# One product for the scores of both batch rows of a tile, and a re-searched issue order

## The chip, the cores and the metric

The kernel runs on one core of a Trainium2 chip. The metric is the time of one launch on the device in microseconds (us). A core has a matrix engine (PE in the profile, with its weight loads listed as PEld), a vector engine (DVE), a scalar engine (ACT), GpSimd (POOL) and a queue engine that issues transfers (SP). Each engine executes its own list of instructions in order, and semaphores hold an instruction back until what it needs is there.

## The reference

Two blocks follow each other. The first is a recurrence over 768 steps, for 4 batches and 8 heads, with a state of 40 x 40:

```python
y[:, :, t] = np.einsum('bhd,bhde->bhe', rt, state)
Sa = np.einsum('bhde,bhe->bhd', state, at)
state_decay = state * wt[:, :, None, :] - np.einsum('bhd,bhe->bhde', Sa, bt)
state = state_decay + np.einsum('bhd,bhe->bhde', vt, kt)
```

Its output, laid out as 3072 tokens of 320 channels, goes through a gated feed-forward block with 1536 inner channels:

```python
xn = x / np.sqrt(np.mean(x * x, axis=-1, keepdims=True) + 1e-06) * rms_g
out = silu(xn @ w_gate) * (xn @ w_val) @ w_out
```

The inputs of the recurrence are float32; everything on the chip is computed in float32.

## The kernel before

**Chunks.** The sequence is cut into 24 chunks of C = 32 steps. For a chunk, `front(c)` loads the inputs, turns them and builds the decayed keys of five levels (blocks of 1, 2, 4, 8 and 16 steps); `inverse(c)` solves a triangular system on DVE; `main(c)` applies the solution, updates the state, forms the chunk's outputs `y` and normalises them. Chunks are collected into 13 groups (one, then eleven times two, then one), and `feed(g)` sends a group's tokens (128 or 256 columns) through the feed-forward weights. `narrow` converts these weights from 64-bit words once, near the start.

**The scores.** A tile of 128 partitions holds two halves. In the turned operands `vut` and `rE` the partition half `o` (partitions 0 to 39 and 64 to 103) and the slot `n` (eight of them) together tell which of 16 sequences of a pair of batches it is, and `i` tells which pair. The two `i` sit side by side along the free dimension, as the two batch rows of a tile, with 64 columns of `vut` for each. The step that the change touches, `pe("score", ...)` in `main`, multiplies for each of the 8 x 2 x 2 combinations of `n`, `i`, `o` a stationary block of `vut` of 40 x 64 by a moving block of `rE` of 40 x 32 (32 time steps), and writes 64 partitions by 32 columns. After it, the levels' masked copies `As` are made from these scores: for each of the five levels, DVE (`tt`) or ACT (`scale`) multiplies the score columns of that level by the mask `msi`. `msi` is indexed by the partition half and by `i`, and is zero where the two don't belong together. The `level` products that follow, 16 for each level, multiply `As` by the keys and give the chunk's own part of `y`.

**Products and records.** A float32 product appears in the profile as two PE records with a weight load each, and a transpose (`flip`) as one with one load. So the 32 products of a chunk's scores are 64 records, 1536 in all. Products whose operands lie on different partition halves, or whose outputs do, work on different tiles of the matrix engine.

**The order.** Nothing is issued where it is written. Each call records a step (`plan.add`) with what it needs, 5999 steps in all, of which 1093 are groups of PE products. At the end `plan.issue(ORDER, PAIRS)` issues all steps in the order of a written list, `ORDER`, each word counting from the first step that is not yet issued. `PAIRS` says which of three pairs of PSUM banks (`ps0` to `ps2`) each use of PSUM gets; a fourth pair, `po`, gathers the feed-forward outputs. On each engine, and on each transfer queue (SP's, POOL's), the list is therefore the order of execution. The list was found by a search outside the kernel.

**Lines in the profile.** Steps are issued through helpers, so the profile's lines are theirs: L531 is every product (`mm`), L534 every transpose (`flip`), L485 the DVE operations, L508, L512 and L515 ACT's, L528 the transfers. The tiles tell steps apart: `ps<-rE,vut` is the scores, `ps<-As,KN` and `ps<-As,kbn` the levels, `ps<-rE,Sd` and `ps<-r,Sd` the state's part of `y`, `ps<-A,K` and `ps<-Ab,K` the products of keys, `ps<-VU,KN` the update of the state, `ps<-xg,wf` and `po<-wf,hT` the feed-forward block, `ps<-ident,...` the transposes.

Of the kernel before, what the change touches and what calls it, by code (L numbers as in the profile page):

```python
# [16 lines left out]
P = 128  # L17
C = 32
# [15 lines left out]
72 66 3 68 69 2 4 200 693 192 46 36 5 6 25 0 0 57 58 195 40 0 53 55 336 51 52 40 63 0 41 69 68 58 359 186 78 79 195  # L34
189 196 46 358 184 379 0 41 0 0 4 45 17 14 16 15 77 367 375 0 0 0 17 18 55 65 47 173 0 18 13 382 360 23 172 56 381
361 675 85 0 351 352 61 353 64 185 173 63 73 76 89 0 76 357 99 4 0 1 21 25 85 70 95 109 97 22 369 370 352 2 86 4 353
0 0 10 362 363 656 165 657 49 3 52 51 80 340 82 357 341 373 58 62 374 346 347 358 67 92 91 359 348 103 366 367 66
360 70 69 63 15 41 40 42 368 349 64 78 77 65 74 94 79 89 88 75 93 85 86 350 59 90 96 97 105 101 76 106 100 108 107
110 167 87 99 649 369 111 351 109 174 175 176 9 156 113 115 114 20 361 352 370 181 375 102 98 22 371 112 385 178 179
182 188 376 377 372 393 192 187 189 193 191 177 204 183 184 378 116 383 403 402 50 289 194 382 117 190 200 384 118  # L40
119 205 120 203 121 163 198 122 123 185 124 199 125 288 126 202 186 127 379 195 211 128 209 129 210 130 380 131 201
215 132 24 405 404 0 169 158 390 210 129 377 420 421 209 130 192 202 204 218 131 203 213 132 391 392 393 133 214 224
134 135 136 223 225 156 222 382 137 138 286 640 212 644 168 139 140 141 142 144 651 394 402 215 383 384 395 385 396
143 227 386 216 397 387 228 226 441 229 403 388 404 405 642 422 423 406 176 424 407 217 289 408 145 440 232 233 425
271 287 641 430 193 643 649 14 659 288 234 235 426 236 429 431 442 272 237 238 239 427 443 149 444 240 219 241 100
242 428 243 221 148 146 664 665 147 273 244 432 433 274 275 434 435 245 445 246 247 446 248 276 277 447 450 451 449
249 452 453 454 250 448 251 436 252 437 253 254 471 472 455 438 255 456 492 281 278 280 491 256 439 482 257 457 258
481 473 279 230 231 290 282 291 650 658 648 646 259 480 474 475 458 260 208 220 261 483 459 283 262 264 265 493 476
494 294 263 302 301 311 299 303 312 295 296 495 763 666 300 298 297 500 501 503 502 477 484 496 304 307 266 0 307
496 673 304 484 269 308 646 485 14 835 819 0 231 46 2 1 0 195 18 22 196 23 186 24 25 469 470 472 368 197 26 187 251  # L50
540 207 371 370 212 198 231 369 381 473 383 375 385 388 376 474 526 525 213 214 27 28 399 386 215 475 476 430 230
398 29 387 410 216 384 217 397 30 396 477 479 481 478 31 480 395 406 530 533 538 539 536 537 250 241 232 218 377 392
378 233 393 394 234 379 484 32 485 252 235 242 240 239 380 389 391 529 527 409 405 408 390 400 407 253 254 364 543 0
0 370 371 203 210 204 368 378 222 384 379 387 389 390 388 393 391 394 392 385 211 205 229 381 212 223 382 380 369
213 455 459 458 383 228 214 224 466 469 516 457 456 215 465 460 462 463 461 468 216 470 225 249 471 464 467 472 398
399 400 401 402 476 403 517 474 0 2 385 403 404 472 476 405 406 407 477 408 409 0 0 395 327 328 396 329 330 331 332
311 312 418 164 428 431 430 429 435 333 334 391 143 142 436 335 336 337 338 339 340 341 545 544 365 415 248 342 343
345 346 344 347 348 349 442 417 446 437 366 397 546 549 548 547 441 529 443 166 167 448 447 438 445 444 439 452 440
456 458 350 351 454 453 457 455 530 449 465 451 414 459 468 464 463 450 146 460 461 469 471 472 482 480 462 467 532
533 434 147 148 470 466 483 481 486 487 168 663 473 149 674 150 151 425 478 534 476 169 152 485 477 484 474 490 424  # L60
535 536 537 170 171 538 539 479 172 173 540 531 475 541 491 492 493 494 495 496 497 498 499 500 369 370 542 676 664
675 681 662 670 665 667 677 671 673 666 543 550 678 551 501 502 503 504 505 506 507 508 509 672 398 399 400 510 680
401 686 511 512 513 687 402 554 555 556 783 185 174 176 514 515 516 517 518 519 520 175 558 177 178 557 523 522 521
524 562 560 563 179 180 564 559 561 181 182 566 565 568 183 184 573 569 567 570 571 525 528 403 527 575 572 574 576
784 577 578 786 186 187 188 579 842 843 841 526 854 580 488 489 682 840 685 844 683 785 189 744 787 788 789 669 697
684 851 839 790 404 581 702 405 407 696 406 190 191 688 192 689 690 847 582 695 700 712 710 713 698 699 724 733 701
791 795 709 711 793 792 583 794 691 798 584 585 721 692 707 693 708 552 694 703 720 732 799 706 719 717 195 194 193
196 197 718 722 723 553 704 714 715 725 729 726 731 705 730 727 716 802 807 728 804 803 736 806 810 813 815 816 805
811 809 198 199 200 0 0 4 6 806 810 815 816 812 584 817 732 733 735 738 820 818 821 5 739 737 736 743 744 745 746
747 1 0 0 737 738 745 746 4 0 0 701 702 773 703 704 628 799 801 797 798 806 617 705 706 774 707 708 770 775 709 776  # L70
777 808 810 952 802 953 811 807 710 814 1078 1075 1082 1073 809 823 1083 711 1085 1072 1074 828 0 0 1087 5 813 0 3 5
0 0 811 4 707 708 822 709 807 808 46 47 48 53 821 816 710 817 819 711 830 52 54 49 712 820 713 0 829 840 0 781 783
782 664 5 665 0 665 790 761 666 762 776 667 670 669 778 777 763 764 773 792 791 789 787 46 0 47 42 43 770 769 44 49
788 783 48 50 45 89 797 663 666 779 781 794 90 780 684 790 791 799 800 798 0 0 0 642 652 710 594 701 384 386 387 1
576 0 10 17 6 785 0 1 650 0 380 700 8 10 573 697 927 638 922 9 2 4 712 11 5 0 698 571 12 14 779 780 782 15 591 592
796 0 792 794 702 700 703 701 568 778 0 0 0 767 768 781 365 769 770 772 773 771 367 366 695 696 697 698 699 700 701
702 703 704 706 705 708 709 710 711 712 713 714 715 716 717 718 719 720 721 722 723 724 725 726 727 728 729 730 0 1
773 782 706 730 602 603 604 605 894 783 370 731 732 733 734 735 736 367 606 372 371 368 373 797 800 799 737 738 739
786 792 740 741 787 788 918 919 905 742 743 744 904 2 789 791 745 369 374 790 793 796 746 798 794 805 795 806 801
912 747 802 748 895 803 804 807 808 809 810 1109 811 914 812 749 1098 1097 0 1102 913 747 748 912 1093 1104 926 931  # L80
749 751 750 752 0 542 546 547 570 558 0 5 0 5 314 550 551 553 554 315 9 0 565 5 6 0 0 552 543 544 561 545 576 558
559 562 564 546 376 378 377 555 557 560 575 574 556 569 570 572 227 573 571 13 595 582 7 12 9 8 10 14 15 566 567 577
578 579 730 568 394 580 585 0 0 0 212 214 213 1 215 379 649 388 389 417 572 570 571 574 575 573 576 418 419 420 524
567 565 421 2 4 580 581 363 585 582 583 587 584 589 586 3 647 648 8 5 591 588 590 593 594 712 505 703 650 592 595
596 597 598 599 600 601 602 364 651 655 653 708 707 704 718 654 7 0 0 0 0 641 647 1 566 592 593 594 595 596 597 598
599 600 601 648 651 657 567 602 656 603 604 605 652 658 606 662 664 665 607 2 7 8 653 4 654 608 655 661 699 504 659
609 660 610 666 611 667 612 9 10 663 668 669 671 670 613 672 614 673 674 615 675 616 676 3 5 617 618 0 671 682 962
487 702 704 6 706 8 613 614 842 0 7 400 698 702 711 610 611 612 613 614 704 615 616 700 617 619 712 705 706 710 715
725 716 618 620 714 959 713 960 958 969 727 723 717 726 707 728 724 9 721 736 708 967 970 838 492 722 709 718 738
737 720 733 719 732 0 6 0 0 0 4 615 617 616 618 728 628 629 723 724 734 735 745 742 743 744 747 749 729 733 737 748  # L90
540 739 746 725 678 688 689 822 395 396 398 397 0 733 731 828 830 747 682 955 829 394 815 816 818 831 957 954 945 0
# [313 lines left out]
def kernel(  # L405
# [41 lines left out]
    N = 8  # L447
    NI = 2 * N
# [38 lines left out]
    def tt(o, a, b, op, more=0.0):  # L487
        dve(0.065, nc.vector.tensor_tensor, o, a, b, op, more=more)
# [359 lines left out]
    def main(c):  # L848
# [61 lines left out]
        for j, l in reversed(list(enumerate(LEVELS))):  # L910
            G = C // (2 * l)
            if G == 1:
                for i in range(2):
                    scale(As[:, j, :, i], sc.rearrange("p o n t -> p (o n) t")[:, :, 16:C], msi[:, j, i, 0:1])
# [183 lines left out]
```

## Time and profile before

| What | Value |
|---|---|
| median of three runs | 1036.21 us (1034.24 to 1039.02) |
| the profiled execution's own time | 1031.24 us |
| its span, first to last instruction | 1029.5 us |
| PE busy | 945.0 us (92%), 24592 products, 24592 weight loads |
| DVE busy | 788.9 us (77%), 2745 instructions |
| ACT busy | 497.8 us (48%), 1113 instructions |
| POOL busy | 301.1 us (29%), 528 instructions |
| mean granted PE clock | 0.952 |
| instruction transfers | 193 packets with 3.16 MB on one queue, 47 with 0.39 MB on another |

A busy PE need not be at its peak: the profile models the end of a product, and a record's length (some 200 ns for a small product) contains time in which the next ones already run. What a group of products costs is therefore read from the start of its first record to the start of the next group's first one.

### The profile page before, as it was taken

The numbers are of one execution on the slowest core, as the hardware profiler recorded it, in microseconds if no ns is written. First come the engines' busy times: TensorE is split into PE (matmuls) and PEld (weight loads), VectorE is DVE, ScalarE is ACT, GpSimd is POOL, SyncE is SP. The second block draws the span as 40 slices with busy tenths as digits, with TensorE's granted clock in tenths as the row PEclk, the third lists the DMA queues.
The fourth block names the chain that finished last, engine by engine and source line by source line (L and its number), as shares of the span: only waits on it lengthen the run. The fifth ranks groups of instructions, "written<-read, shape, count | busy, mean of one in ns | idle before, by whom it ended". The sixth has DMA issues, their size and how long they took to land.

```text
span 1029.5 us, 55521 instructions
## 1 busy us (share of the span) xinstructions
PE 945.0 (92%) x24592; PEld 770.9 (75%) x24592; DVE 788.9 (77%) x2745; ACT 497.8 (48%) x1113; POOL 301.1 (29%) x528
## 2 busy tenths in 40 slices
PE   3557878999999999999999899999999999999998
PEld 2446767877777778777877777777787787787777
DVE  8999977966869778878878678688698788777531
ACT  5676456554463454464454534634534545436131
POOL 9323234211433232333321324123232313400000
PEclk9996555999999999999999999999999999999999
DMA  7664433322242242232331233232322322420100
GB/s 167 152 175 107 109 87 79 61 60 54 47 83 43 49 88 48 55 79 44 67 77 28 60 65 60 55 67 45 78 48 54 78 47 60 75 44 10 42 7 21
DMA packets 147056, 68.89 MB, mean 67 GB/s; under 512 B 121088, under 2 KB 136384, under 8 KB 146816
## 3 DMA queue, kind: packets, MB, share of 16 engines
q1 hardware_dynamic: 128448, 42.37, 18.3%
q0 software_dynamic: 16192, 22.64, 11.5%
q8 instruction: 193, 3.16, 1.3%
q10 hardware_dynamic: 2176, 0.33, 0.2%
q14 instruction: 47, 0.39, 0.1%
HBM read 55.05 MB, written 10.22 MB: 63 GB/s over the span
## 4 chain that ended last, share of the span: by engine, by line
PE 78%; DVE 6%; DMA 6%; issue 5%; SPq 3%; ACT 2%; POOL 0%; DVEq 0%; ACTq 0%; POOLq 0%
PE ps L531 55%; PE po L531 16%; PE ps L534 7%; SPq L528 3%; DMA sB<-LT 1%; DMA M<-sB 1%; DVE Yi L485 1%; DMA LT<-sY 1%; ACT VU L512 1%; DVE wf L485 1%; DVE y L485 1%; DVE tmp L485 1%; DVE LT L485 1%; DMA kbn<-in_b_dram 1%; DMA sY<-Yi 1%
## 5 line engine op out<-in xcount | busy, mean ns | idle before, releaser
L531 PE MATMUL ps<-xg,wf 128*128 128x256 f32 (+3 forms) x1872 | 360.8, 375 | 0.0
L531 PEld LDWEIGHTS ps<-xg,wf 128*128 128x128 f32 (+1 forms) x1872 | 267.7, 190 | 48.7 <-issue 12.5
L531 PE MATMUL po<-wf,hT 128*128 128x320 f32 x576 | 180.8, 448 | 1.5 <-issue 1.3
L531 PEld LDWEIGHTS po<-wf,hT 128*128 128x128 f32 x576 | 103.5, 191 | 38.8 <-issue 4.5
L485 DVE TENSOR_TENSOR hT<-ps,sg 128x256 f32<-128x256 f32 (+1 forms) x156 | 59.9, 399 | 91.0 <-PE ps L531 54.8
L485 DVE TENSOR_TENSOR tmp<-Yi,M 128x24 f32<-128x24 f32 (+21 forms) x512 | 106.9, 209 | 16.8 <-ACT x L508 3.3
L485 DVE TENSOR_TENSOR Yi<-Yi,tmp 128x24 f32<-128x24 f32 (+21 forms) x512 | 106.9, 209 | 10.6
L508 ACT ACTIVATE sg<-ps 128x256 f32<-128x256 f32 (+1 forms) x156 | 54.0, 369 | 110.0 <-PE ps L531 107.0
L528 POOL DMA_DIRECT2D VU<-in_v_dram x92 | 54.1, 590 | 154.0 <-PE ps L531 113.8
L485 DVE TENSOR_TENSOR K<-K,T 128x512 f32<-128x512 f32 (+1 forms) x192 | 92.6, 497 | 4.8 <-PE ps L531 2.7
L531 PE MATMUL ps<-Ab,K 40*60 40x56 f32 (+2 forms) x4608 | 83.3, 232 | 8.6 <-DVE tmp L485 2.4
L531 PEld LDWEIGHTS ps<-Ab,K 40*60 40x60 f32 (+2 forms) x4608 | 76.1, 143 | 17.1 <-issue 8.3
L518 POOL TENSOR_TENSOR ss<-ss,mhalf 128x1 f32<-128x1 f32 x24 | 14.3, 596 | 249.8 <-DVE ss L485 249.7
L512 ACT COPY KN<-ps 128x640 f32<-128x640 f32 x96 | 65.8, 692 | 39.0 <-DVE LT L485 24.7
L528 POOL DMA_DIRECT2D kbn<-in_k_dram x92 | 53.9, 587 | 100.5 <-PE ps L531 99.3
L485 DVE TENSOR_TENSOR As<-ps,msi 128x256 f32<-128x256 f32 (+1 forms) x168 | 70.9, 454 | 15.5 <-PE ps L531 8.7
L528 POOL DMA_DIRECT2D kbn<-in_b_dram x92 | 53.8, 586 | 82.5 <-PE ps L531 80.8
L531 PEld LDWEIGHTS ps<-As,KN 128*40 128x40 f32 x3072 | 67.5, 129 | 12.6 <-issue 4.2
L531 PE MATMUL ps<-As,KN 128*40 128x32 f32 x3072 | 72.7, 208 | 3.5 <-DVE As L485 1.6
L512 ACT COPY K<-K 128x512 f32<-128x512 f32 x96 | 61.0, 635 | 28.6 <-PE ps L531 13.3
L485 DVE SCALAR_TENSOR_TENSOR Yi<-M,Yi 128x31 f32<-128x31 f32 (+6 forms) x228 | 44.4, 243 | 30.8 <-DMA M<-sB 18.5
L528 POOL DMA_DIRECT2D wn<-in_w_dram x92 | 51.8, 564 | 45.3 <-DVE KN L485 45.1
(128 smaller groups left out, 1503.8 us busy)
## 6 DMA issues: line engine op xcount, KB each, us to landing
M<-sB SPq DMA_DIRECT2D x96, 128.0 KB, 3.0
wan<-in_r_dram SPq DMA_DIRECT2D x24, 160.0 KB, 3.7
kbn<-in_k_dram POOLq DMA_DIRECT2D x92, 40.0 KB, 2.4
kbn<-in_b_dram POOLq DMA_DIRECT2D x92, 40.0 KB, 2.8
VU<-in_v_dram POOLq DMA_DIRECT2D x92, 40.0 KB, 3.0
wan<-in_w_dram POOLq DMA_DIRECT2D x46, 80.0 KB, 2.9
wan<-in_a_dram POOLq DMA_DIRECT2D x46, 80.0 KB, 2.8
wn<-in_w_dram POOLq DMA_DIRECT2D x92, 40.0 KB, 2.7
```

What stands on the lines that cost most here:

```text
L485: plan.add("DVE", time + more + each * size(o), 0.087, lambda at: [fn(at(o), *m(at))], [o], aps(*args))
L508: scalar(o, [a], lambda at: nc.scalar.activation(at(o), at(a), f, **kw), aps(acc), 0.1 if f in (AF.Square, AF.Relu) else 0.0)
L512: scalar(o, [a], lambda at: nc.scalar.copy(at(o), at(a)), extra=more)
L518: plan.add("POOL", 0.5, 0.06, lambda at: nc.gpsimd.tensor_tensor(o, a, b, op), [o], [a, b])
L528: plan.add(by, 0.6 if by == "POOL" else 0.45, 0.0, lambda at: queue.dma_start(out=o, in_=i), [o], [i], load=load, since=since)
L531: return o, lhsT, rhs, lambda at: nc.tensor.matmul(at(o), lhsT, rhs, start=start, stop=stop, skip_group_check=True), 4
L534: return o, i, ident, lambda at: nc.tensor.transpose(at(o), i, ident), 2
```

## The change

Two things change, the score products and the written order. The five masked copies read the same number of elements as before, now at the place where the new product puts them.

A score product now takes both batch rows of a slot together: the stationary operand is all 128 columns of `vut` (40 x 128), the moving operand the 2 x 32 steps of both rows (40 x 64), and the output 128 partitions by 64 columns. There are 8 x 2 of them in a chunk in place of 8 x 2 x 2. Half of each output block pairs a partition half with the other row's steps; these cross blocks are finite numbers that nothing needs, and the zeros of `msi` remove them.

```diff
         sc = plan.room().rearrange("p o (n t) -> p o n t", n=N)
-        pe("score", [mm(sc[half(i), o, n, 0:C], vut[part(o), n, half(i)], R["rE"][part(o), n, i, tk])
-                          for n, i, o in each])
+        pe("score", [mm(sc[:, o, n].rearrange("p (i t) -> p i t", i=2), vut[part(o), n], R["rE"][part(o), n, :, tk])
+                     for n in range(N) for o in range(2)])
+        sc = sc.rearrange("p o n (i t) -> p (o n) i t", i=2)
         As = As_.next()
         for j, l in reversed(list(enumerate(LEVELS))):
             G = C // (2 * l)
             if G == 1:
                 for i in range(2):
-                    scale(As[:, j, :, i], sc.rearrange("p o n t -> p (o n) t")[:, :, 16:C], msi[:, j, i, 0:1])
+                    scale(As[:, j, :, i], sc[:, :, i, 16:], msi[:, j, i, 0:1])
             elif l == 1:
-                tt(As[:, j], sc.rearrange("p o n t -> p (o n) t")[:, :, None, 1:C:2].to_broadcast((P, NI, 2, 16)),
+                tt(As[:, j], sc[:, :, :, 1::2],
                    msi[:, j:j + 1].to_broadcast((P, NI, 2, 16)), MUL)
             else:
                 for i in range(2):
                     tt(As[:, j, :, i].rearrange("p n (g l) -> p n g l", g=G),
-                       side(sc.rearrange("p o n t -> p (o n) t")[:, :, 0:C], l, 1),
+                       side(sc[:, :, i], l, 1),
                        msi[:, j:j + 1, i].rearrange("p n (g l) -> p n g l", g=G).to_broadcast((P, NI, G, l)), MUL)
```

The lists `ORDER` and `PAIRS` are replaced as a whole, by the result of a new search; in it the time of an order was a mean over several assumed delays of the blocks in which instructions arrive. The 5999 steps are the same, but for the size of the 24 score steps; only their order and the PSUM pairs differ.

```diff
 ORDER = """
-72 66 3 68 69 2 4 200 693 192 46 36 5 6 25 0 0 57 58 195 40 0 53 55 336 51 52 40 63 0 41 69 68 58 359 186 78 79 195
+71 46 2 4 72 368 200 3 202 0 53 190 54 52 46 4 5 50 6 49 7 78 69 66 76 77 67 0 53 0 38 42 191 194 39 51 55 77 78 357
...
```

## The prediction

> **What bounds the kernel now.** I read the page's busy shares and slices first, then the sums over stretches, PE's waits, and the order of time on PE.
>
> ```profile
> PE 945.0 (92%) x24592; PEld 770.9 (75%) x24592; DVE 788.9 (77%) x2745; ACT 497.8 (48%) x1113; POOL 301.1 (29%) x528
> ...
> PE   3557878999999999999999899999999999999998
> ...
> DVE  8999977966869778878878678688698788777531
> ...
> PEclk9996555999999999999999999999999999999999
> ```
>
> ```profile
> core 0: us, PE busy (x) PEld busy (x) DVE busy (x) ACT busy (x) POOL busy (x), PEclk, DMA share, GB/s
> 0.00:193.00 193.00, 131.12 (x4282) 118.32 (x4282) 168.94 (x507) 113.94 (x227) 76.31 (x145) 0.75 0.52 121
> ...
> 200.00:1000.00 800.00, 781.95 (x19900) 626.31 (x19899) 609.90 (x2196) 374.95 (x859) 219.68 (x375) 1.00 0.27 56
> ```
>
> There are two stages. Up to 193 us DVE is the busiest (168.9 of 193), PE has 61.9 us idle, and its granted clock is mostly half. From 200 to 1000 us PE is busy 782 of 800: work added to PE there moves the end, and at most 18 us of its idle time could take some up. Of these 18 us the waits of a quarter microsecond or more sum to 13.2 for "issue", with nothing in the profile to wait for, and 2.7 for ACT, DVE or DMA. Over the whole span the largest wait is:
>
> ```profile
> PE ps L531 <- issue: 12.9, 19, 1.6
> ```
>
> Last, the order of time on PE at full clock (start, time to the last end, records):
>
> ```profile
> 304.79 0.22 PE L531 MATMUL ps<-rE,Sd 40*40 40x32 f32 x1
> ...
> 305.42 1.11 PE L531 MATMUL ps<-rE,vut 40*64 40x32 f32 x64
> 306.47 4.79 PE L531 MATMUL ps<-xg,wf 64*128 64x256 f32 x24
> ...
> 322.17 1.15 PE L531 MATMUL ps<-A,K 40*64 40x56 f32 x64
> 323.14 1.06 PE L531 MATMUL ps<-Ab,K 40*60 40x56 f32 x64
> ...
> 346.93 1.14 PE L531 MATMUL ps<-rE,vut 40*64 40x32 f32 x64
> 347.89 0.20 PE L531 MATMUL ps<-rE,Sd 40*40 40x32 f32 x1
> ...
> 358.40 0.70 PE L534 MATMUL ps<-ident,K 40*128 40x40 f32 x16
> 359.03 1.13 PE L531 MATMUL ps<-xg,wf 128*128 128x256 f32 x4
> ```
>
> ```profile
> 1003.09 1.16 PE L531 MATMUL ps<-xg,wf 64*128 64x128 f32 x16
> ```
>
> Read from start to next start, 64 records of the scores (40 x 64 stationary, 32 moving columns) take 346.93 to 347.89 = 0.96 us, or 1.05 us at 305.42. The group of y's state part before them has 64 records too, and 32 moving columns, but 40 stationary ones: 304.79 to 305.42 = 0.63 us. The keys' product has 64 stationary and 56 moving columns: 322.17 to 323.14 = 0.97 us. So moving 32 or 56 columns is the same, and 40 or 64 stationary ones is the difference: such groups are bound by loading the stationary operand. The score records start in rounds of four (one for each quarter of the engine) 0.0585 us apart.
>
> **The change part by part.**
>
> 1. The scores' product. A chunk's 64 records become 32, with 128 stationary and 64 moving columns. An output of 128 partitions leaves two tiles (the partition halves), so it is 16 rounds of two in place of 16 rounds of four. The nearest row is the last fence: 64 x 128 stationary, the same two tiles, 128 moving columns; its pairs start 0.112 us apart, and the 16 records hold PE for 1.09 us until the next group's start. Its weight-load records are 0.188 us long against the scores' 0.135, so the load is longer by 0.053, as a round is (0.112 against 0.0585). Sixteen rounds at 0.112 are 1.79 us; with 0.06 for the first I take 1.85. Lower end: transposes of 40 x 128, 16 records in 358.40 to 359.03 = 0.63 us, so 1.26 for 32; but a transpose's load record is 0.138 us, and an ordinary product's isn't. Upper end: the group of 16 twice, 2.18. So +0.86 us a chunk at full clock (from 0.99, the mean of 0.96 to 1.05; +0.27 to +1.19). Twenty of the 24 score groups start after 200 us: +17.2 us (5 to 24).
>
> 2. The first four, at 70, 102, 146 and 176 us, run at half clock, where the group at 146 took 1.87 us; twice +0.86 is 1.7 each, 6.9 in all if nothing covers it, nothing if DVE does. DVE covers most of this stage, so I take +2.
>
> 3. The masked copies. DVE's rows of 256 and 512 elements (416 and 681 ns) and ACT's (471 ns) keep their sizes; only the address changes. Zero, and I see no row that would price a stride. They wait for the scores, 0.9 us longer each; the wait is hidden while PE has other groups to run, as it has after 200 us, and lies on the chain at the first chunks (in 2).
>
> 4. Changes of tile shape. The scores took 0.954 us where the next group has the same tile shape, and 1.044 to 1.066 where it hasn't: 0.1 us a change. Counted in the two written orders, PE goes from 530 changes to 557, since the scores leave the shape of y's products for that of the transposes: +2.7 us.
>
> 5. Blocks of instructions. 193 packets for PE's 49184 records and some 280 others are 256 instructions each, and the "issue" gaps after 200 us fall on every 256th instruction. They come where the 256 before took, by the rows of their groups, under about 3.1 us, and last about what is missing. Summed so, 29 blocks after 200 us lack 18.2 us; the trace shows 18.3 lost at block ends (13.2 of idle, the rest records that start late). In the new order it is 187 blocks, and 30 short ones that lack 20.0 us. I take 0, from -13 (all idle of this kind gone) to +5.
>
> 6. The rest of the order. The steps are the same 5999. Ahead of each score and each group's first feed-forward product stand the same sums of PE work, within 2.6 us, and in the first 200 us of DVE work, within 2 us; nothing is moved by a stage. SP's and POOL's transfers are reshuffled in their queues: POOL waits hundreds of us in all and PE for a transfer hardly at all after 200 us, so that costs nothing unless a load comes late for a turn (9.5 us, once, near 16 us in this trace). Nothing, -6 to +6.
>
> 7. Longer scores give the other engines time: of the 4.8 us (18 less 13.2) in which PE waited for others, I let 4 go.
>
> Sum: 17.2 + 2 + 2.7 + 0 + 0 - 4 = +17.9 us, or 1049 on the profiled execution's own 1031.24. That one is 5 us below the median of the runs, so I add the sum to 1036.21: 1054 us.
>
> **The rivals.**
>
> *The count rules (faster).* If each record cost the same, 32 in place of 64 would halve the group: 0.5 us x 24 = -12, so 1024 us. It decides if the new group takes under 0.96 us. Against it: 0.63 and 0.97 us for equal counts. The Trainium skill states this rule, in "TensorEngine Tiling (Array Packing)", Instruction Overhead: each product carries some 60 cycles, whatever its few moving columns, so a small size should not be split. The trace agrees as to the moving columns (32 or 56: 0.96 and 0.97 us), but not that the records' count alone sets the time. Chance 0.04.
>
> *The load is that of a transpose.* Then +0.27 x 20, with 2.7 for shapes and less for 7: +5, 1041 us. Against it: the load records of 0.188. Chance 0.06.
>
> *The new order wins the time back*, at block ends and at the start: to hide 17 us nearly all of the 18.3 must go. For it: that is what its search averaged over. Against it: 20.0 us by the rows. 1037 us, chance 0.13.
>
> *The clock.* It is granted for good at 193 us. PE is busy 46.5 of 50 us from 150 to 200, so each 10 us that full clock comes earlier there are worth up to 5 us. Granted near 120 us it would give some 30 us, 1024 us (chance 0.06); granted 40 us later, 1074 us (0.05). Longer score groups fill gaps, which may help; no row settles it.
>
> **How the numbers follow.** Forecast 0.66, alone 1044 to 1066 us (items 1 and 5). A change under 0.5% (5 us, about what these runs can tell from none) takes most of the winning order (0.10 of 0.13) and the transposes' load (0.06), less a little: same 0.15. Faster: 0.04 + 0.06 + a tail of 0.01: 0.11. Slower 0.74. The range from 1035 to 1070 leaves out the count, the two clocks and a part of the winning order, 0.18.
>
> **What would show it.** The group `ps<-rE,vut` has 768 records of 40*128 with 64 moving columns, starting in pairs 0.112 us apart and taking 1.8 to 2.0 us to the next group's start; DVE's and ACT's `As` rows are as before; PE's span from 200 us on grows, its share of "issue" waits stays near 13 us. The prediction is wrong if that group takes under 1.3 us, if "issue" waits fall below 5 us, or if the clock is granted far from 193 us.

## The result: 1064 us after 1037, slower by 2.75%, and the profile after

| | before | changed |
|---|---|---|
| median of six runs each, side by side | 1036.97 us (1033.29 to 1039.02) | 1064.43 us (1061.28 to 1071.07) |
| ratio, with its 95% interval | | 1.0275 [1.0239, 1.031] |
| the same, in later runs | 1035.34 us | 1060.87 us, 1.0253 [1.0201, 1.0306] |
| own time and span of the profile read here | 1031.24 and 1029.5 us | 1053.92 and 1052.1 us |

The forecast was 1054 us, +17.9; the medians say +27.5 and +25.5. The first profile of the changed kernel ran at a granted clock of at most 0.949 throughout (span 1069.3 us), so the lines below come from the second, `e0_changed_again`, whose full clock is 1.0. It is the fastest of that kernel's four runs there, by 4.7 us or more, so it holds only part of what the medians show: its span is 22.6 us longer than before's.

From the page of the changed kernel, the busy sums and the 40 slices:

```profile
PE 967.0 (92%) x23824; PEld 792.1 (75%) x23824; DVE 795.1 (76%) x2745; ACT 500.8 (48%) x1113; POOL 303.4 (29%) x528
...
PE   2547888999999999999999999999999999999998
...
DVE  9989998867867867768778688678597687776531
...
PEclk9997665999999999999999999999999999999999
```

PE executes 768 records fewer and is busy 22.0 us longer (967.0 against 945.0), of the 22.6 us by which the span has grown. DVE, ACT and POOL are within 6.2, 3.0 and 2.3 us of before. The sums over stretches (length, then busy time and records of PE, PEld, DVE, ACT, POOL, then granted clock, share of the transfer engines, GB/s):

```profile
0.00:193.00 193.00, 129.28 (x4108) 117.39 (x4110) 172.18 (x496) 112.49 (x222) 76.95 (x143) 0.80 0.50 120
...
200.00:1000.00 800.00, 782.47 (x19048) 629.63 (x19049) 603.85 (x2185) 372.49 (x848) 222.39 (x378) 1.00 0.26 55
1000.00:1053.00 53.00, 48.22 (x598) 39.05 (x596) 12.54 (x36) 12.10 (x35) 0.56 (x1) 1.00 0.07 15
```

From 200 to 1000 us PE was as idle as before: 17.5 us of 800 against 18.1. Longer products did not take up its waits. The largest waits of PE, over the whole span (engine, line, what it waited for: us, times, longest; lines here are one lower than in the kernel before):

```profile
PE ps L533 <- DVE wf L484: 11.6, 1, 11.6
PE ps L530 <- issue: 9.6, 13, 1.7
```

Now the group itself, in the order of time on PE (start, time to the last end, records), and its records by tile (shortest, median, longest in ns), first in the changed kernel:

```profile
308.02 1.98 PE L530 MATMUL ps<-rE,vut 40*128 40x64 f32 x32
309.84 1.08 PE L530 MATMUL ps<-xg,wf 64*128 64x256 f32 x8
```

```profile
L530 PEld LDWEIGHTS ps<-rE,vut x768: 182/188/331, 76.2 to 1014.2; 40*128 40x128 f32 x192
L530 PE MATMUL ps<-rE,vut x768: 258/272/472, 76.2 to 1014.3; 40*128 40x64 f32 x192
```

and the loads in the kernel before:

```profile
L531 PEld LDWEIGHTS ps<-rE,vut x1536: 129/135/228, 70.4 to 990.4; 40*64 40x64 f32 x192
```

Half the records take 1.82 us (308.02 to 309.84), and 1.93 where the next group has another tile shape (390.87 to 392.80), in place of 0.96 to 1.05: the load of 128 columns is 188 ns against 135. The rows of the masked copies (mean ns of one after the bar's busy time) stay where they were, 416, 681 and 471 ns before:

```profile
L484 DVE TENSOR_TENSOR As<-ps,msi 128x256 f32<-128x256 f32 x144 | 55.6, 417 | 31.4 <-ACT As L514 22.8 <-PE ps L530 8.5
...
L484 DVE TENSOR_TENSOR As<-ps,msi 128x512 f32<-128x512 f32 x24 | 16.4, 683 | 2.4 <-PE ps L530 1.8 <-ACT As L514 0.6
...
L514 ACT ACTIVATE As<-ps,msi 128x256 f32<-128x256 f32 x48 | 21.0, 471 | 46.7 <-PE ps L530 33.5 <-DVE As L484 13.2
```

### The profile page after: what moved, and what is told of

Its sections match the earlier page's. It is cut to its first block, busy times and chain, and to the rows that moved or that the text cites. A ratio compares the mean times of both kernels' runs of the same rounds, so it can differ in the third digit from the quotient of the medians.

```text
span 1069.3 us, 53960 instructions
## 1 busy us (share of the span) xinstructions
PE 983.4 (92%) x23824; PEld 797.2 (75%) x23824; DVE 796.2 (74%) x2745; ACT 502.1 (47%) x1113; POOL 303.9 (28%) x528
## 4 chain that ended last, share of the span: by engine, by line
PE 77%; DVE 8%; DMA 5%; ACT 4%; issue 4%; SPq 1%; POOL 1%; DVEq 0%; ACTq 0%; POOLq 0%
PE ps L530 55%; PE po L530 15%; PE ps L533 6%; SPq L527 1%; ACT VU L511 1%; DVE Yi L484 1%; DVE y L484 1%; DMA sB<-LT 1%; DMA M<-sB 1%; DVE tmp L484 1%; DVE LT L484 1%; DVE K L484 1%; DMA wf<-in_moe_w_out_dram 1%; DVE As L484 1%; DMA kbn<-in_k_dram 1%
## 5 line engine op out<-in xcount | busy, mean ns | idle before, releaser
L530 PE MATMUL ps<-xg,wf 128*128 128x256 f32 (+3 forms) x1872 | 373.8, 385 | 0.3 <-DVE hT L484 0.3
L530 PEld LDWEIGHTS ps<-xg,wf 128*128 128x128 f32 (+1 forms) x1872 | 272.1, 193 | 53.9 <-issue 10.9
L530 PE MATMUL po<-wf,hT 128*128 128x320 f32 x576 | 186.9, 461 | 0.8 <-issue 0.7
L517 POOL TENSOR_TENSOR ss<-ss,mhalf 128x1 f32<-128x1 f32 x24 | 16.8, 698 | 166.2 <-DVE ss L484 165.8
```

Source lines behind the costliest of these rows:

```text
L517: plan.add("POOL", 0.5, 0.06, lambda at: nc.gpsimd.tensor_tensor(o, a, b, op), [o], [a, b])
L530: return o, lhsT, rhs, lambda at: nc.tensor.matmul(at(o), lhsT, rhs, start=start, stop=stop, skip_group_check=True), 4
```

## The experiments

The theory: a float32 product with few moving columns costs what loading its stationary columns costs, so that the score groups pay 0.86 us each; changes of tile shape pay 0.1 us; the order's other effects come to nothing. The rivals left: that the wider moving operand costs, that the new order is better and hides part of the price, and that the places of the short instruction blocks decide what the order costs.

### The changed kernel again, and its two halves

The first run repeats the changed kernel as it is.

> The changed kernel once more, for a profile at full granted clock: its first profile was granted 0.949 of full clock from 199 us on, the one of the kernel before 1.0. Expected: ratio 1.024 to 1.031 to the kernel before, as measured; with the clock at 1.0 from about 195 us the score group takes 1.83 to 1.94 us from its start to the next group's start, and PE's busy time is some 20 us more than before (965), not 983.

Measured: 1060.87 us (1053.92 to 1063.4), ratio 1.0253 [1.0201, 1.0306]. After 200 us the score groups take 1.81 to 1.93 us, and PE is busy for 967.0.

The score product alone, with the `ORDER` and `PAIRS` of before:

```diff
-        pe("score", [mm(sc[half(i), o, n, 0:C], vut[part(o), n, half(i)], R["rE"][part(o), n, i, tk])
-                          for n, i, o in each])
+        pe("score", [mm(sc[:, o, n].rearrange("p (i t) -> p i t", i=2), vut[part(o), n], R["rE"][part(o), n, :, tk])
+                     for n in range(N) for o in range(2)])
+        sc = sc.rearrange("p o n (i t) -> p (o n) i t", i=2)
...
-                    scale(As[:, j, :, i], sc.rearrange("p o n t -> p (o n) t")[:, :, 16:C], msi[:, j, i, 0:1])
+                    scale(As[:, j, :, i], sc[:, :, i, 16:], msi[:, j, i, 0:1])
```

> The order and the PSUM pairs of before, with the new score product. My theory (the wide load sets the price of a score group, 0.96 to 1.85 us, 20 groups on the bound stretch): +17 to +22 us, ratio 1.017 to 1.021. Rival, the wider product is nearly free and the new order is what costs: ratio under 1.008. Rival, the product costs all of the measured 27 us, with the order neutral: 1.024 to 1.030.

Measured: 1052.64 us (1051.76 to 1055.22), ratio 1.0189 [1.0152, 1.0226]. The group, on PE's order of time:

```profile
304.94 2.00 PE L531 MATMUL ps<-rE,vut 40*128 40x64 f32 x32
306.77 1.50 PE L531 MATMUL ps<-xg,wf 64*128 64x256 f32 x9
```

The new order alone, with the score product of before:

```diff
 ORDER = """
-72 66 3 68 69 2 4 200 693 192 46 36 5 6 25 0 0 57 58 195 40 0 53 55 336 51 52 40 63 0 41 69 68 58 359 186 78 79 195
+71 46 2 4 72 368 200 3 202 0 53 190 54 52 46 4 5 50 6 49 7 78 69 66 76 77 67 0 53 0 38 42 191 194 39 51 55 77 78 357
...
```

> The new order and PSUM pairs, with the score products of before. My theory has the order cost what is left of the 27 us, +5 to +10 us (0.1 us for each of 23 more changes of tile shape, 2.3; short instruction blocks that lack 22.5 us in place of 18.2 by the rows, 4.3; the start): ratio 1.005 to 1.010. Rival, the new order by itself is better, and the wide product hides it: ratio under 0.997. Rival, the order is neutral: 0.998 to 1.003.

Measured: 1045.5 us (1039.71 to 1052.25), ratio 1.0109 [1.0063, 1.0155]. That is a little above what was expected. The two halves multiply to 1.0189 x 1.0109 = 1.030, and the whole gave 1.0275 and 1.0253: within their intervals they add. So about 19.6 us (1.89% of 1036) are the product's. The order costs about 11 by its own run, and 6 to 8 by what the product leaves of the whole. That the new order is better and hides something is refuted; it costs.

Since the order of `e1_score_only` is that of before, its time can be followed chunk by chunk against before's. These are sums over stretches from one score group's start to another's, the fifth to the tenth and the 21st to the end, before and then with the new product:

```profile
225.90:422.60 196.70, 190.99 (x4974) 152.78 (x4962) 154.54 (x557) 94.23 (x216) 60.01 (x103) 1.00 0.29 60
...
859.60:1029.50 169.90, 164.51 (x3342) 131.60 (x3330) 96.69 (x333) 60.74 (x152) 18.19 (x31) 1.00 0.15 31
```

```profile
228.40:425.70 197.30, 194.84 (x4800) 156.88 (x4791) 155.18 (x558) 94.17 (x217) 60.15 (x103) 1.00 0.28 59
...
870.10:1050.10 180.00, 172.06 (x3211) 137.70 (x3199) 97.68 (x337) 60.76 (x152) 18.17 (x31) 0.98 0.14 29
```

All five stretches, worked out the same way (idle is length less PE's busy time; half clock from the granted clock, counted at half its time; a score group is put at 0.86 us dearer, which the groups of the two profiles bear out, see item 1 below):

| score groups | longer by | five, four, ... x 0.86 | idle | time lost at half clock | sum of the three |
|---|---|---|---|---|---|
| start to the 5th | 2.5 | | | | |
| 5th to 10th | 0.6 | 4.3 | -3.3 | 0 | 1.0 |
| 10th to 14th | 0.1 | 3.4 | -1.8 | -1.7 | -0.1 |
| 14th to 18th | 0.9 | 3.4 | -1.2 | 0 | 2.2 |
| 18th to 21st | 6.4 | 2.6 | +1.7 | +1.7 | 6.0 |
| 21st to the end | 10.1 | 3.4 | +2.6 | +3.6 | 9.6 |

Halfway through, PE's idle time does shrink and nearly the whole price seems to be hidden; the last third gives it back. With half as many score records, every later instruction stands at another place in its block of 256 (the blocks in which instructions arrive, below), and the waits at block ends move: over the first three of these stretches (5th to 18th group) they fall from 13.9 to 6.6 us, and over the last two they rise from nothing to 4.7. What stays at the end is the price of the groups (17.2), the 2.5 us of the first four, 2.0 us less of idle time, and 3.6 us for two more falls of the clock (below): 21.3 in all, where the span grew by 20.6.

### Which side of the product is paid for

Moving columns doubled, stationary ones left at 64 (32 products as before, each with the time steps of both rows; the readers of the scores take their half):

```diff
-        pe("score", [mm(sc[half(i), o, n, 0:C], vut[part(o), n, half(i)], R["rE"][part(o), n, i, tk])
+        pe("score", [mm(sc[half(i), o, n].rearrange("p (i t) -> p i t", i=2), vut[part(o), n, half(i)], R["rE"][part(o), n, :, tk])
                           for n, i, o in each])
+        sc = sc.rearrange("p o n (i t) -> p (o n) i t", i=2)
```

> The order of before, 32 score products with the stationary operand of before (40 x 64) and the wide moving one (64 columns, both batch rows). If the load of the stationary columns sets the price, the group keeps 0.95 to 1.07 us and the ratio is 0.998 to 1.003. Rival, the moving columns (twice as many) set it: 1.3 us or more, +8 us or more, ratio over 1.008.

Measured: 1034.09 us over ten runs, ratio 1.0013 [0.9981, 1.0046].

```profile
307.57 1.14 PE L531 MATMUL ps<-rE,vut 40*64 40x64 f32 x64
308.64 1.55 PE L531 MATMUL ps<-xg,wf 64*128 64x256 f32 x9
```

1.07 us for the group against 1.05: twice the moving columns are free.

The reverse: 16 products with all 128 stationary columns and only 32 moving ones. The second batch row's scores are left out of the computation here.

```diff
-        pe("score", [mm(sc[half(i), o, n, 0:C], vut[part(o), n, half(i)], R["rE"][part(o), n, i, tk])
-                          for n, i, o in each])
+        pe("score", [mm(sc[:, o, n, 0:C], vut[part(o), n], R["rE"][part(o), n, 0, tk])
+                          for n in range(N) for o in range(2)])
```

> The order of before, 16 score products with all 128 columns of vut stationary and only 32 moving columns (the steps of the first batch row, whose scores then stand for both rows: the scores of the second row are left out). If the stationary columns alone set the price, the group takes 1.83 to 1.95 us, as with 64 moving columns, and the ratio is that of the score change alone, 1.015 to 1.022. Rival, the product of stationary and moving columns sets it: the group takes about 1.0 us and the ratio is 0.998 to 1.004.

Measured: 1061.03 us (1057.76 to 1064.64), ratio 1.0276 [1.0232, 1.032].

```profile
306.52 1.98 PE L531 MATMUL ps<-rE,vut 40*128 40x32 f32 x32
308.33 0.90 PE L531 MATMUL ps<-xg,wf 64*128 64x256 f32 x6
```

The group takes 1.81 us, as with 64 moving columns. So the stationary columns set the price, as the theory says: 1.82 / 16 = 0.114 us for a round of two, 0.0585 for one of four with half the columns. The columns count at an unchanged number of tiles too: on the same four, 40 take 0.63 / 16 = 0.039. The Trainium skill has the rule in "TensorE: Matmul & The Clock Gate", LDWEIGHTS (loading the stationary operand): a load takes its number of columns, divided by 1.2, in ns. By an estimate from it, 128 and 64 columns would take 107 and 53 ns, and the traces agree within 10%.

But the kernel is 8 us slower than `e1_score_only`, which has the same order and the same group time, and that the theory did not foresee. Its profile shows five falls of the clock to half, each one 3.4 us, in the part where the clock is otherwise full. One of them, as a sum over three stretches (the clock is the third number from the end of a row) and PE's order of time ahead of it:

```profile
551.00:554.10 3.10, 3.10 (x96) 2.86 (x85) 2.75 (x13) 1.52 (x5) 0.00 (x0) 1.00 0.00 0
554.10:557.50 3.40, 3.40 (x8) 2.20 (x7) 3.06 (x10) 0.27 (x1) 0.00 (x0) 0.50 0.03 5
557.50:561.00 3.50, 3.50 (x102) 3.00 (x103) 1.02 (x5) 0.00 (x0) 0.00 (x0) 1.00 0.00 0
```

```profile
551.51 1.98 PE L531 MATMUL ps<-rE,vut 40*128 40x32 f32 x32
553.41 2.40 PE L531 MATMUL po<-wf,hT 128*128 128x320 f32 x5
```

PE never waits in the stretch ahead: 3.10 busy of 3.10. Four of the five falls are of this kind; each follows within 3.1 us the start of a group that loads 128 columns for 32 moving ones. The fifth follows a wait of 1.6 us. The mean granted clocks of the timed runs agree: span times (1 - clock), the time lost if all of it were PE's, is 57.7 us over its four runs and 50.5 over the six of `e1_score_only`. That is 7.2 of the 8.0 us between their mean spans.

### The places of the instruction blocks

Counted in the traces, all the idle time of PE after 200 us that is put down to "issue" stands at the end of a block of 256 instructions (of waits of a quarter microsecond or more, 13.2 us in before, 13.2 in the changed kernel, and none elsewhere). If the sum over the groups' rows prices these blocks, as the prediction assumed, moving all blocks by some instructions must move the time. 28, 46 or 40 products of 32 x 32 into unused columns of `po` were put behind the first PE group; each is four instructions, so they shift the rest by 112, 184 and 160:

```diff
-... 359 186 78 79 195
+... 359 186 78 - - - (28 or 46 of them) 79 195
...
-    plan.warm = lambda: nc.tensor.matmul(po_[:, 0, DM:DM + P], ident, ident, start=False, stop=False, skip_group_check=True)
+    plan.warm = lambda: nc.tensor.matmul(po_[0:32, 0, DM:DM + 32], ident[0:32, 0:32], ident[0:32, 0:32], start=False, stop=False, skip_group_check=True)
```

> The kernel of before with 28 tiny products (112 instructions, about 1 us while PE waits for its first loads) right after the first group on PE: every block of 256 PE instructions ends 112 instructions earlier in the work. By the rows of the groups the short blocks after 200 us lack 13.0 us in place of 18.1: ratio 0.993 to 0.998, with PE's waits for issue near 9 us. Rival, the issue waits have nothing to do with where blocks end: ratio 0.999 to 1.003 and the waits stay at 13 us, not on every 256th instruction.

> The same with 46 tiny products (184 instructions): by the rows the short blocks lack 27.5 us in place of 18.1: ratio 1.005 to 1.012, PE's waits for issue near 20 us after 200 us. Rival, as for the other shift: 0.999 to 1.003.

The 40 words for the changed kernel stand behind its own first PE group.

> The changed kernel with 40 tiny products (160 instructions): by the rows the short blocks lack 9.2 us in place of 20.0, so some 10 us less than the changed kernel: ratio 1.013 to 1.018 to the kernel before. Rival, the place of the blocks' ends does not matter: 1.024 to 1.030.

Measured: 1034.23 us, ratio 1.0016 [0.9991, 1.0041], with the shift of 112; 1049.11 us, 1.0139 [1.0093, 1.0186], with 184; and 1065.5 us, 1.0316 [1.0279, 1.0352], for the changed kernel with 160. Two misses, and one whose sign alone was right. PE's "issue" waits from 200 us on, in before and then with each shift (the last is the changed kernel, whose row without a shift has 9.1):

```profile
PE ps L531 <- issue: 11.4, 15, 1.6
```

```profile
PE ps L532 <- issue: 10.4, 14, 1.5
...
PE ps L535 <- issue: 2.7, 3, 1.3
```

```profile
PE ps L532 <- issue: 15.2, 16, 1.9
```

```profile
PE ps L531 <- issue: 9.6, 12, 2.3
```

The waits are real and always at block ends, but the sum by rows forecast changes of -5.1, +9.4 and -10.8 us at those ends, and the traces show about -0.5, +3.2 and -1.6 (late records included). The rows of groups do not say how long a block lasts to that precision. With 184 most of the rest is the clock: five windows (of 3.4 us) at half clock after 200 us against one, 4 x 1.7 = 6.8 us. With 3.2 of "issue" waits and 2.9 of PE's other idle time this makes 12.9 of the 16.1 us by which its span grew. The 46 products themselves cost nothing that can be seen: the fifth score group starts at 225.93 us, and at 225.94 before.

### What a change of tile shape costs

One product of 32 x 32 was put in the middle of each of the 156 output steps of the feed-forward block, which raises the changes of tile shape from 530 to 832; then two such products in a row, which leaves the changes at 832:

```diff
-                pe("out", [mm(po[:, q, 0:DM], hTs[:, e, q * P:(q + 1) * P], wfs[e][:, 2 * P:2 * P + DM], f + e == 0, f + e == FT - 1)
-                                            for q in range(GROUPS[g])])
+                outs = [mm(po[:, q, 0:DM], hTs[:, e, q * P:(q + 1) * P], wfs[e][:, 2 * P:2 * P + DM], f + e == 0, f + e == FT - 1)
+                        for q in range(GROUPS[g])]
+                outs[1:1] = [mm(po[0:32, 0, DM:DM + 32], ident[0:32, 0:32], ident[0:32, 0:32], False, False)] * 1
+                pe("out", outs)
```

> The kernel of before with one tiny product (32 x 32 stationary, 32 moving columns, into unused columns) in the middle of each of the 156 steps of the output product: 302 more changes of tile shape on PE (530 to 832). If a change costs 0.1 us, +30 us for the changes and +3 to +7 us for the products: ratio 1.025 to 1.040. Rival, changes of shape are free: +3 to +7 us, 1.003 to 1.007.

> The same with two tiny products in a row in each place: the changes of tile shape stay 832, the tiny products double. The difference to the run with one is the price of the products alone: +3 to +7 us, ratio some 0.005 above it. Rival, changes are free and the products are dear: the difference to the run with one is as large as that run's own difference to the kernel before.

Measured: 1086.23 us, ratio 1.0492 [1.0432, 1.0553], and 1099.42 us, 1.0646 [1.0574, 1.0717]; both above what was expected. One such step on PE's order of time, with one product (two records) and with two:

```profile
303.85 0.81 PE L531 MATMUL po<-wf,hT 128*128 128x320 f32 x2
304.59 0.24 PE L531 MATMUL po<-ident 32*32 32x32 f32 x2
304.76 0.54 PE L531 MATMUL po<-wf,hT 128*128 128x320 f32 x1
```

```profile
300.04 0.81 PE L531 MATMUL po<-wf,hT 128*128 128x320 f32 x2
300.77 0.31 PE L531 MATMUL po<-ident 32*32 32x32 f32 x4
301.01 0.81 PE L531 MATMUL po<-wf,hT 128*128 128x320 f32 x2
```

A step of four output records takes 1.181 us in before (median, start to the next start), 1.552 with one product between and 1.615 with two. The second product costs 0.063, so the two changes cost 1.552 - 1.181 - 0.063 = 0.308, 0.15 each. By the times it is about 0.12: the ratios make +51 us for one product and +67 for two, the second thus 16, and (51 - 16) / 302 = 0.12. Part of the difference is waiting that the longer work on PE took up: PE's idle time after 200 us is 11.6 us with one product, against 18.1 before. The Trainium skill says in "TensorEngine Tiling (Array Packing)", Key Properties, that changing the tiling mode drains the engine. The traces agree in that a change costs time, and give this price for 128 x 128 to 32 x 32 and back; the draining itself is not seen in them.

## Why the prediction was right, and where it was wrong

**Item 1, the scores' product: right.** In `e1_score_only` the 20 groups after 200 us take 1.78 to 1.93 us, 37.7 together. Before they take 0.95 to 1.07 where no wait falls into them, some 20.6 together: 17.1 us more, where 17.2 was forecast. It is partly luck that the two agree so closely: both ends of the step, 1.85 and 0.99, were 0.04 too low (1.89 and 1.03 on average), as most of the groups, before and after, are followed by a change of tile shape. The row of the feed-forward product with 64 x 128 stationary columns was the right one to take. Both rivals on the product fall with it: fewer records did not help, and neither the transposes' shorter load nor the moving columns (`e3_wide_moving`, `e4_narrow_moving`) set the time.

**Item 2, the first four groups: in keeping, but not shown.** +2 forecast; the fifth score group starts 2.5 us later in `e1_score_only`. In `e3_wide_moving` and `e5_before_shift112`, whose groups cost what they did before, it starts 2.0 and 2.2 us later too, so single profiles do not tell this term from their scatter.

**Item 3, the masked copies: right.** 417, 683 and 471 ns.

**Item 4, changes of tile shape: right, the term perhaps a little small.** +2.7 forecast at 0.1 us each. Counted on PE's order of time, the changes are 530 before, 553 in `e2_order_only` and 557 in the changed kernel. At the 0.12 to 0.15 us of a change to 32 x 32, the 27 would cost 3.2 to 4.0; that is an estimate, as these changes are between other shapes.

**Item 5, instruction blocks: the value right, the way to it wrong.** 0 was forecast, and "issue" idle after 200 us is 13.6 us in the changed kernel against 13.9 before. But the step priced blocks by the sums of their groups' rows, and the three shifts showed that these sums miss by 5 to 9 us. The bounds of -13 to +5 had no such ground.

**Item 6, the rest of the order, taken as nothing with bounds of -6 to +6: too low, by how much is not settled.** The order alone costs about 11 us (lower end of its interval 6.5), of which shapes are 2 to 3; some 8 us are left, outside the bounds. By what the product leaves of the whole, 6 to 8 us, 3 to 6 are left, inside them. In the profile of `e2_order_only`, 8.4 us longer than before's, one sees 1.1 us lost up to the fifth score group, +0.7 us of idle after 200 us and two more falls of the clock (2 x 1.7 = 3.4); with 2 to 3 for shapes this makes 7 to 8. But the mean granted clock of its six timed runs is 0.952, as in before's 41 (0.952), so that the falls are not shown to be the steady part; the profile is also the fastest of the six runs. Where the order's remaining time goes in the other five stays open.

**Item 7, -4 us for longer scores covering other waits: wrong.** PE's idle time from 200 to the end, for "issue" and others, is 13.9 + 4.2 us before, 11.3 + 5.1 with the new product alone and 13.6 + 3.9 in the changed kernel. Of the whole 0.5 to 1.6 us went, not 4, and of the waits for others 0.3 at most: with the product alone they even grew.

**The sum.** 17.2 + 2 + 2.7 = 21.9 without the absorption that was not there, and 3 to 8 of the order that were not in it: 25 to 30, against 25.5 and 27.5 by the medians. So the step that failed is item 7, and item 6 was too low; both err to the same side, which is why the time lies nearer the upper end (1070) than the forecast. The increase is half as large again as the forecast one, and the range holds it because it was wide.

**The clock.** The prediction said that full clock is granted for good at 193 us. Counted from the span's start as all other times here, it is 182.8 us; the step misread the origin, which moved no term. In the changed profile it is 186.0 us. Of the three signs that should have made it wrong (a group under 1.3 us, "issue" under 5 us, a far grant) none came.

## What to carry to other kernels

For small float32 products, count the columns of the stationary operand that each engine tile must load: 40, 64 and 128 of them took 0.63, 0.96 and 1.82 us for groups of 64, 64 and 32 records, and for 64 and 128 it made no difference whether 32 or 64 columns moved past. Merging two products along the stationary side halved the records and saved nothing here, and it loses where the merged output needs all partitions and leaves two tiles busy in place of four. An order that is searched for must be timed on its own, with the old arithmetic, before the two are put together, and gains read off half a trace may be given back in the other half.

## What the runs showed that was not expected

**The clock is decided on a fixed grid, and short waits suffice to lose it.** In all twelve profiles (before, two of the changed kernel, the nine other experiments) all changes of the granted clock lie whole multiples of 3413.3 ns apart: in before the grant at 182.82, the fall at 578.77 and the return at 582.18 us are 116.0 and 117.0 steps apart. That fall, as sums over two stretches and on PE's order of time:

```profile
575.00:578.80 3.80, 2.41 (x161) 2.12 (x162) 3.20 (x13) 1.47 (x4) 2.22 (x4) 1.00 0.31 67
578.80:582.20 3.40, 3.40 (x66) 2.52 (x66) 2.99 (x14) 2.13 (x6) 3.40 (x7) 0.50 0.49 101
```

```profile
577.06 0.26 PE L531 MATMUL ps<-Xs,LT 32*32 32x40 f32 x3
578.71 1.05 PE L531 MATMUL ps<-Xs,LT 32*32 32x40 f32 x50 [1.39 <-issue]
```

A wait of 1.39 us for instructions ended at 578.71, and the next step of the grid, 3.4 us long, ran at half clock: 1.7 us more. Cut into steps of that grid from 200 us on, the twelve profiles have some 2930 at their full clock. The next one was at half clock after 9 of 10 in which PE was idle for 1.6 us or more, 10 of 30 with 1.2 to 1.6, 5 of 122 with 0.5 to 1.2, none of 125 with 0.2 to 0.5, and 4 of some 2640 below; those four are the ones of `e4_narrow_moving`. A block-end wait of 1.4 us can therefore cost 1.4 us or 3.1, by where it falls on the grid. The grid stands elsewhere against the work in each profile, which would explain part of the spread between runs; over the 41 runs of the kernel before, span and mean clock go together (correlation -0.65).

The Trainium skill, "TensorE: Matmul & The Clock Gate", What's actually happening, describes such a free-running window of 3413 ns, and the traces agree in its length to the nanosecond. It names an idle window as what takes the full clock away; here 24 falls followed steps with only 0.8 to 2.1 us of idle time, and four followed steps with next to none.

**Four falls of the clock had no wait ahead of them.** They came behind groups with 128 stationary and 32 moving columns. But eleven more such groups lay whole within a step of the grid, and no fall followed. Of the same groups with 64 moving columns 33 lay whole within a step (in both profiles of the changed kernel, `e1_score_only` and `e7_changed_shift160`), and none had a fall behind it. So the number of moving columns probably matters, but what sets the four steps apart from the eleven, and whether loading counts as idle for the clock, stays open.
